# A long convolution by FFT beside a state-space scan on one core: the inner FFT stages in smaller array pieces, with real and imaginary parts on the same partition

## The chip, the cores and the metric

One core of one Trainium2 chip. The time is device microseconds of one launch. The profile that is quoted is one execution of its own: its span is the time from its first to its last instruction, and its device time stands beside it in the table.

## What is computed

Two independent layers on sequences of S = 2048 rows and D = 1024 channels; their outputs stand side by side in the last dimension.

```python
# layer A (H3): shift convolution, gate, long convolution through an FFT, gate
k_shift = sum(k_pad[:, t:t + S, :] * shift_k[:, 3 - t] for t in range(4))
kv = k_shift * v
y  = irfft(rfft(kv, 2 * S) * rfft(ssm_k, 2 * S))[:S] + kv * ssm_D
a  = q * y
# layer B (S5): a diagonal complex state-space model, P = 1024 states
Bu = x @ B_bar.T;   h[t] = Lam_bar * h[t - 1] + Bu[t]
b  = 2 * real(h @ C.T) + x * Dskip
out = concatenate([a, b], -1)
```

## The kernel before

All of the kernel's work is cut into small tasks with short names (`U`, `am`, `sh`, ...), functions in the table `E`. One long string, `ORDER`, lists about 1240 calls of them (`am.4.1` is `am(4, 1)`). The program is issued in just that order: it is the order on each engine's queue. After a colon the string names the buffers that a task takes: `p0`, `p1` (one PSUM bank each), `d0` to `d2` (PSUM tiles of two banks), `b`, `a` (SBUF ring buffers of 2 and 4 KB a partition), `m` (a product buffer), `e` (`hab`, in three copies), `w` (weights `wts`, in two copies). `@G` puts a transfer on GpSimd's queue in place of SyncE's, `@S` the other way, `@D` a copy on VectorE in place of ScalarE.

Layer B. `bl` loads blocks of B, `bT` transposes them on TensorE (L458), `bc` copies them to SBUF. `x` and `cx` load `x` and C through transposing transfers on SyncE (L483, L480). For each of 16 chunks of 128 rows, `U` multiplies with B (L492, 2048 matmuls of 128 columns), `ue` evicts, and VectorE runs a chain that cannot be split between chunks: `r1` (rotate), `r2` (add), `sc` (scan, L523), `cm` (carry), `r3`, `r4`. Then `y` multiplies with C (L546, 512 columns), with the skip term at L551, `ye` evicts and `yst` stores. Before all that the small tasks `p32` to `par_rest`, `z1`, `stt`, `rt` make tables from Lambda and dt.

Layer A. The FFT has length 4096 = 128 x 32, half of the input being zero padding.
- `kp`, `vp` load k and v; `kvm`, `kva`, `kvb`, `kvc` form kv on VectorE (L583 to L604). `wb`, `wbe` make the shift weights.
- First stage: `am` (L610) multiplies kv with the DFT matrix `F1t`, two matmuls of 128x128 by 512 columns, `ae` evicts, `ast` stores to the DRAM buffer `Ys_kv`. For the filter: `hl` loads, `hT` transposes, `hm` (L643) multiplies, `he`, `hst` store to `Ys_h`.
- Second stage, for 16 groups `gq` of two frequencies: `lh`, `lk` load from the DRAM buffers, `lw` the weights. `sh`, `sk` (`s2`, L676) multiply, `she`, `ske` evict into `hab` and `x16`. The real part of a frequency then lies on 32 partitions, the imaginary part on the next 32. `sw` makes a copy of `hab` with the two exchanged: four SBUF-to-SBUF transfers of 32 partitions. `pr` (L704) multiplies both copies with `x16` on VectorE. `sa` (L717) combines the products and does the inverse second stage in the same matmuls, `sae` evicts, `vst` stores to `Vs`.
- Last stage: `vl` loads from `Vs`, `a3` (L744) multiplies with `Gt`, `a3e` evicts, `qm` multiplies with q (loaded by `qp`), `ost` stores.

`s2` and `sa` work on pieces of 64 rows by 64 columns of the array: `tile_position` gives the piece, and four pieces with different weights can be at work together. All other matmuls use the whole array. A partition holds a block of 16 rows of the sequence, in order. Half of the entries of `F1t` and `Gt` are zero, since even and odd blocks are transformed apart from each other.

Of the kernel before, what the change touches and what calls it, by code (L numbers as in the profile page):

```python
# [18 lines left out]
MAGIC = 12582912.0  # L19
# [8 lines left out]
def a_constants():  # L28
# [13 lines left out]
    WF = np.zeros((2, N2, 2, 32, 3, N2))  # L42
# [3 lines left out]
    WF[:, :, :, :, 2, :] = WF[:, :, :, :, 0, :]  # L46
    WI = np.zeros((2, 2, N2, 16, 2, 2, N2, 2))
    for gi in range(2):
        for ui in range(2):
            for gq in range(16):  # L50
                cc = np.transpose(c_[ui, 2 * gq + gi], (1, 0)); ss = np.transpose(s_[ui, 2 * gq + gi], (1, 0))
                o = WI[gi, :, :, gq, ui]
                o[0, :, 0, :, 0] = cc; o[0, :, 0, :, 1] = ss
                o[1, :, 0, :, 0] = -cc; o[1, :, 0, :, 1] = -ss
                for cp in range(2):
                    o[cp, :, 1, :, 0] = -ss; o[cp, :, 1, :, 1] = cc
    W = np.concatenate([WF.reshape(128, NWP, 4 * 96), WI.reshape(128, NWP, 2 * 256)], axis=2)
    f = lambda a: np.ascontiguousarray(a.reshape(128, -1), dtype=np.float32).astype(ml_dtypes.bfloat16)
    return f(F1), f(G1), f(W)
# [3 lines left out]
NA = 11  # L63
# [3 lines left out]
ld_par bl.4.0@G:b0 bl.5.0@G:b1 bl.5.1@G:b2 bl.4.1:b3 bl.6.0:b4 bl.2.1@G:b5 ld_sd@S bl.1.1@G:b6 ld_w@S:a0a1 kp.0@G kp.-2 ld_F par_T:p0 hl.2@G:a2  # L67
bl.7.0:b7 bT.4.0:p1 p32 exp1 bl.6.1:b8 hl.3@G:a3 bc.4.0 dve2 x.0:b9 kp.-1@G bT.5.0:p0 dve3 sm_pre bT.4.1:p1 bc.5.0 hl.1@G:a4 bl.0.1:b10 bc.4.1
bl.7.1@G:b11 x.4:b12 bT.6.0:p0 tabA1:a5a6a7a8 bc.6.0 bl.2.0:b13 hl.0:a9 exp2 bl.0.0:b0 sin0 rt@G kp.1 bT.1.1:p1 x.2:b1 bT.5.1:p0 tabA2 bc.1.1 cx.4.1
wb.7:p1 bc.5.1 par_rest vp.0@G:a10 ld_G@S sin2 wb.4:p0 cx.5.1 wbe.4 sin1 wb.6:p0 cx.0.0 wbe.6@D eo.0 bl.3.1:b3 wb.1:p0 wbe.7@D bl.1.0:b4 wbe.1@D  # L70
wb.2:p1 cx.0.1 eo.1 stt.0 wb.0:p0 cx.7.0 wbe.2 stt.1 eo.3 wb.5:p1 bl.3.0:b6 x.1:b2 wbe.5@D wbe.0 stt.3 wb.3:p1 wbe.3 bT.6.1:p0 cx.1.0 dd bT.2.0:p1
kvm.0:m0 vp.1:a1 vp.2:a0 cx.6.0 bc.6.1 cx.6.1 bT.0.1:p0 bc.2.0 bc.0.1@D kp.2@G eo.2 bT.2.1:p1 kva.0 hT.0.0:p0 hc.0.0:b8 stt.2 bc.2.1 hT.0.1:p0
bT.7.1:p1 hc.0.1:b13 kvb.0:a7 bc.7.1 hT.0.6:p0 hm.0.0.1:d0 kvc.0 hc.0.6:b10 hT.0.3:p1 hm.0.0.0:d1 kvm.4:m0 he.0.0.1:b5 am.1.1:d2 hc.0.3:b11
hm.0.6.1:d0 hst.0.0.1 hT.0.2:p0 bT.0.0:p1 he.0.6.1:b8 hc.0.2:b0 hst.0.6.1@S cx.1.1 bc.0.0 bT.7.0:p0 bc.7.0@D cx.3.1 z1 U.0.3.0:p1 kva.4 hm.0.6.0:d0
U.0.3.1 cx.3.0 U.0.2.0:p0 kvb.4:a8 U.0.2.1 ue.0.3:a10 he.0.6.0:b7 kvm.2:m0 bT.1.0:p1 bc.1.0 am.0.1:d0 bT.3.0:p1 ue.0.2 bc.3.0 bT.3.1:p0 bc.3.1
U.0.0.0:p1 U.0.0.1 he.0.0.0:b5 kp.4@G kva.2 kp.3@G ae.0.1:b10 hm.0.3.1:d1 U.2.2.0:p0 ue.0.0 ast.0.1@S vp.4:a5 kvc.4 U.0.1.0:p1 ae.1.1:b4 cx.5.0
# [70 lines left out]
def full_kernel(ctx, tc, A_q, A_k, A_v, A_shift_k, A_ssm_k, A_ssm_D, B_x, B_Lre, B_Lim, B_Bre, B_Bim,  # L147
# [676 lines left out]
```

## Time and profile before

| | |
|---|---|
| Device time, median of 3 runs | 378.24 us (374.16 to 381.8) |
| Device time of the profiled execution | 380.41 us |
| Its span | 378.5 us |
| TensorE busy (matmuls) | 346.6 us (92%) |
| VectorE busy | 324.6 us (86%) |
| ScalarE busy | 264.2 us (70%) |
| GpSimd busy | 81.3 us (21%) |
| DMA | 100.06 MB in 67418 packets, 264 GB/s |

A busy share is a mean over the whole span. Busy times of matmuls are those of overlapping instructions with modelled ends: for the pace of a stream, starts are compared with starts. Where a row of the timeline ends in brackets, the first number is how long the engine sat idle before the row, and behind the arrow stands what it waited for. The granted TensorE clock was 1.00 throughout.

### The profile page before, as it was taken

The page shows a single profiled execution, that of the slowest core. Times are in us where ns is not written, and L with a number is a line of the kernel's source. Part 1 is how long each engine was busy: PE and PEld are TensorE (multiplying, and loading weights), DVE is VectorE, ACT ScalarE, POOL GpSimd, SP SyncE. Part 2 cuts the span into 40 slices and gives each one's busy share as a digit, 9 for nine tenths or more (in the row PEclk, how much of TensorE's full clock was granted, in tenths as well). Part 3 has the DMA queues.
Part 4 walks back from the last instruction along what each step waited for, and adds up shares of the span by engine and source line. Part 5 has one row for each costly group of instructions (what it writes and reads, how often), then busy time and mean ns, then how long its engine had stood idle before and what let it go on. Part 6 is the DMA issues. An engine that isn't in the chain of part 4 may idle for free.

```text
span 378.5 us, 8748 instructions
## 1 busy us (share of the span) xinstructions
PE 346.6 (92%) x3661; PEld 225.6 (60%) x3661; DVE 324.6 (86%) x229; ACT 264.2 (70%) x341; POOL 81.3 (21%) x150
## 2 busy tenths in 40 slices
PE   4548889899899999999999999989999999999995
PEld 3226678785455578855444757367867664467442
DVE  6989599999999997999997797576899999993972
ACT  4978798877778886952785879778869771346433
POOL 7300023022112521214200325330210202211021
PEclk9999999999999999999999999999999999999999
DMA  6999999997578999999999897999989539877995
GB/s 231 317 338 216 265 272 286 296 314 235 200 243 270 247 313 287 281 272 268 190 275 312 258 324 234 220 267 221 284 236 312 175 125 325 306 229 255 350 319 206
DMA packets 67418, 100.06 MB, mean 264 GB/s; under 512 B 38435, under 2 KB 42147, under 8 KB 67380
## 3 DMA queue, kind: packets, MB, share of 16 engines
q1 hardware_dynamic: 54660, 56.32, 54.8%
q0 software_dynamic: 12720, 43.19, 36.8%
q8 instruction: 28, 0.46, 0.5%
q14 instruction: 10, 0.08, 0.1%
HBM read 49.16 MB, written 33.55 MB: 219 GB/s over the span
## 4 chain that ended last, share of the span: by engine, by line
PE 56%; DMA 15%; issue 13%; ACT 7%; SPq 4%; POOL 2%; DVE 1%; POOLq 0%; ACTq 0%; DVEq 0%
PE ps_u L492 22%; PE ps_y L546 16%; PE ps_a L744 4%; DMA wts<-a_c_W 4%; SPq L483 4%; DMA Ys_kv<-ysb 3%; PE ps_a L643 3%; DMA l2k<-Ys_kv 3%; DMA ld<-in_B_B_re_dram 3%; PE ps_a L717 3%; PE ps_a L610 3%; DMA hab<-hab 2%; PE ps_a L676 2%; PE ps_t L630 2%; ACT ysb L615 2%
## 5 line engine op out<-in xcount | busy, mean ns | idle before, releaser
L492 PEld LDWEIGHTS <-BT 128*128 128x128 bf16 x2048 | 119.3, 98 | 22.6 <-issue 11.7
L492 PE MATMUL ps_u<-xT,BT 128*128 128x128 bf16 x2048 | 127.7, 219 | 2.4 <-ACT u L497 1.2
L546 PE MATMUL ps_y<-CT,h 128*128 128x512 bf16 x512 | 127.7, 379 | 0.0
L546 PEld LDWEIGHTS <-h 128*128 128x128 bf16 x512 | 44.6, 98 | 48.0 <-issue 6.1
L523 DVE TENSOR_TENSOR_SCAN h<-rtab,h 128x2080 bf16<-128x2080 f32 x16 | 71.8, 4488 | 0.2
L497 ACT CAST u<-ps_u 128x512 bf16<-128x512 f32 x64 | 38.2, 603 | 27.0 <-PE ps_u L492 19.1
L506 DVE TENSOR_TENSOR mt<-u,Z 128x4096 bf16<-128x4096 bf16 x16 | 36.7, 2291 | 15.8 <-ACT u L497 15.4
L704 DVE TENSOR_TENSOR hab<-x,hab 128x4096 bf16<-128x4096 bf16 x16 | 36.5, 2286 | 15.2 <-DMA hab<-hab 10.5
L556 ACT CAST yo<-ps_y 128x512 bf16<-128x512 f32 x32 | 19.1, 596 | 28.0 <-PE ps_y L546 24.4
L650 ACT CAST ysbh<-ps_a 128x1024 bf16<-128x1024 f32 x32 | 32.3, 1033 | 8.8 <-PE ps_a L643 7.5
L691 ACT CAST x<-ps_a 128x1024 bf16<-128x1024 f32 x32 | 31.9, 1026 | 8.8 <-PE ps_a L676 5.9
L506 DVE TENSOR_TENSOR mt<-h,Z 128x4096 bf16<-128x4096 bf16 x16 | 36.7, 2292 | 0.5
L724 ACT CAST vsb<-ps_a 128x1024 bf16<-128x1024 f32 x32 | 31.7, 1027 | 6.5 <-PE ps_a L717 6.0
L583 DVE TENSOR_TENSOR mt<-kring,wbc 128x2048 bf16<-128x2048 bf16 (+3 forms) x14 | 35.8, 2592 | 0.4 <-ACT wbc L473 0.2
L615 ACT CAST ysb<-ps_a 128x1024 bf16<-128x1024 f32 x32 | 32.3, 1043 | 2.7 <-issue 1.6
L685 ACT CAST hab<-ps_a 128x1024 bf16<-128x1024 f32 x32 | 32.2, 1030 | 2.1 <-PE ps_a L676 1.9
L551 PE MATMUL ps_y<-Dd,xT 128*128 128x128 bf16 x128 | 28.0, 219 | 0.0
L749 ACT CAST ot<-ps_a 128x1024 bf16<-128x1024 f32 x16 | 15.7, 1018 | 14.1 <-PE ps_a L744 14.1
L169 POOL DMA_DIRECT2D Ys_h<-ysbh x20 | 14.3, 716 | 43.3 <-ACT ysbh L650 43.3
L168 POOL DMA_DIRECT2D hab<-hab x32 | 15.6, 494 | 32.1 <-ACT hab L685 18.3
L458 PE MATMUL ps_t<-ident,ld 128*128 128x128 bf16 x128 | 13.9, 285 | 9.1 <-DMA ld<-in_B_B_re_dram 4.4
L643 PE MATMUL ps_a<-hT,F1t 128*128 128x512 bf16 x64 | 20.6, 402 | 0.8 <-ACT ysbh L650 0.6
(116 smaller groups left out, 381.8 us busy)
## 6 DMA issues: line engine op xcount, KB each, us to landing
Ys_h<-ysbh POOLq DMA_DIRECT2D x20, 256.0 KB, 5.5
l2h<-Ys_h SPq DMA_DIRECT2D x9, 512.0 KB, 9.7
Vs<-vsb SPq DMA_DIRECT2D x9, 512.0 KB, 4.3
vv<-Vs SPq DMA_DIRECT2D x9, 512.0 KB, 5.2
Ys_kv<-ysb POOLq DMA_DIRECT2D x17, 256.0 KB, 6.2
l2k<-Ys_kv SPq DMA_DIRECT2D x8, 512.0 KB, 3.9
hab<-hab SPq DMA_DIRECT2D x32, 128.0 KB, 5.4
l2k<-Ys_kv POOLq DMA_DIRECT2D x8, 512.0 KB, 7.8
```

The costliest lines, as they stand in the source:

```text
L492: nc.tensor.matmul(pu[:, w, jl, :], BT[:, 2 * jp + jl, w, d, :], xT[:, d, :], start=(d == 0), stop=(d == ND - 1))
L497: nc.scalar.copy(u[:, :, 2 * jp:2 * jp + 2, :], st["pu", i, jp][:])
L506: nc.vector.tensor_mul(m, s_, w_)
L523: nc.vector.tensor_tensor_scan(gf, rtab[:].rearrange("p a j t -> p (a j t)"), gf, 0.0, ALU.mult, ALU.add)
L546: nc.tensor.matmul(py[:], h[:, 1 - w, j, 2:TP], CT[:, j, w, dh * 512:(dh + 1) * 512], start=(j == 0 and w == 0), stop=(j == NJ - 1 and w = ...
L583: nc.vector.tensor_mul(m[:, :, j0:j0 + n, :], a_, wbc[:, j0:j0 + n, :].unsqueeze(1).to_broadcast([P, 2, n, DV]))
L615: nc.scalar.copy(st["ysb", r, u][:], st["pa", r, u][:].rearrange("p e d -> p (e d)"))
L643: nc.tensor.matmul(pd[:, e, :], F1t[:, u, :], st["hT", f, rp][:, e, :], start=True, stop=not sk)
L650: nc.scalar.copy(st["yh", f, rp, u][:], st["pa", f, rp, u][:])
L685: nc.scalar.copy(hab[:, a, :, e * 512:(e + 1) * 512], st["ps", key, gq, e][:])
L691: nc.scalar.copy(x16[:, :, e * 512:(e + 1) * 512], st["ps", "k", gq, e][:])
L704: nc.vector.tensor_mul(hab, x16.unsqueeze(1).to_broadcast([P, 2, 2 * D]), hab)
```

## The change

The blocks of 16 rows are now put on partitions by parity: even blocks on partitions 0 to 63, odd blocks on 64 to 127. `am` so needs only the nonzero halves of its matrix, in pieces of 64x64; `a3` uses pieces of 128 rows by 64 columns. In the second stage a matmul of `s2` gives the real or the imaginary part alone, in pieces of 64 rows by 32 columns, so that both parts of a frequency lie on the same partition (in different places of it). `pr` forms the four products from that, `sw` is gone, and `sa` combines four products in place of two, in pieces of 32 rows by 64 columns, both halves of the channels in one task with two PSUM tiles. Transfers whose rows are split by parity become two of 64 partitions (`kp`, `vp`, `qp`, `ost`), and `vl` is two tasks. The weight tile `wts` grows from 896 to 1024 columns. The small parameter tasks work on real and imaginary parts together, in fewer operations. There is one more ring buffer `a` (`NA` 12 for 11; the row `sd` moves into a `b` buffer), and `ORDER` is a new string throughout.

```diff
-NA = 11
+NA = 12
 ...
-    F1t = const.tile([P, 2, P], BF16, name="F1t")
-    Gt = const.tile([P, 2, P], BF16, name="Gt")
+    F1t = const.tile([P, 384], BF16, name="F1t")
+    Gt = const.tile([P, 2, 64], BF16, name="Gt")
-    kr = k.rearrange("(n s) d -> n s d", s=NR)
+    kr = k.rearrange("(n h s) d -> h n s d", h=2, s=NR)      # vr, qr, oar in the same way
 ...
     def vp(r):
         st["v", r] = k4("v", [P, 2, D])
-        spd(st["v", r][:], vr[:, 2 * r:2 * r + 2, :])
+        for h in range(2):
+            spd(st["v", r][64 * h:64 * h + 64, :, :], vr[h, :, 2 * r:2 * r + 2, :])   # kp, qp, ost in the same way
 ...
-    def am(r, u):
-        for e in range(2):
-            nc.tensor.matmul(pd[:, e, :], F1t[:, u, :], kvt(r)[:, r % 2, e * 512:(e + 1) * 512], start=True, stop=True)
+    def am(r, e):
+        for h in range(2):
+            hp = slice(64 * h, 64 * h + 64)
+            for u in range(2):
+                nc.tensor.matmul(pd[64 * u:64 * u + 64, h, :], F1t[hp, 256 + 64 * u:320 + 64 * u],
+                                 kvt(r)[hp, r % 2, e * 512:(e + 1) * 512], start=True, stop=True, tile_position=(64 * h, 64 * u))
 ...
-    def s2(key, nm, gq, e, o):
+    def s2(key, nm, gq, ri):
         for gi in range(2):
-            for u in range(2):
-                up = slice(64 * u, 64 * u + 64)
-                b0 = ((2 * gq + gi) % 4) * 96 + 32 * o
-                nc.tensor.matmul(pd[64 * gi:64 * gi + 64, u, :], wt[up, b0:b0 + 64],
-                                 st[nm, gq][up, gi, e * 512:(e + 1) * 512], start=True, stop=True,
-                                 tile_position=(64 * u, 64 * gi))
+            b0 = ((2 * gq + gi) % 4) * 64 + 32 * ri
+            for e in range(2):
+                c_ = 32 * (2 * gi + e)
+                for u in range(2):
+                    up = slice(64 * u, 64 * u + 64)
+                    nc.tensor.matmul(pd[c_:c_ + 32, u, :], wt[up, b0:b0 + 32], st[nm, gq][up, gi, e * 512:(e + 1) * 512],
+                                     start=True, stop=True, tile_position=(64 * u, c_))
 ...
-    def sw(gq):
-        hab = st["hab", gq]
-        for b in range(4):
-            o = b ^ 1
-            spd(hab[32 * b:32 * b + 32, 1, :, :], hab[32 * o:32 * o + 32, 0, :, :])
 ...
     def pr(gq):
-        nc.vector.tensor_mul(hab, x16.unsqueeze(1).to_broadcast([P, 2, 2 * D]), hab)
+        nc.vector.tensor_mul(hab, hab[:, :, 1:2, :].to_broadcast([P, 2, 2, D]), x16.unsqueeze(1).to_broadcast([P, 2, 2, D]))
 ...
-    def sa(gq, e):
-        for a in range(2):
-            for u in range(2):
-                for gi in range(2):
-                    gp = slice(64 * gi, 64 * gi + 64)
-                    b0 = 4 * 96 + (gq % 2) * 256 + u * 128 + a * 64
-                    nc.tensor.matmul(pd[64 * u:64 * u + 64, gi, :], wt[gp, b0:b0 + 64],
-                                     hab[gp, a, u, e * 512:(e + 1) * 512], start=(a == 0), stop=(a == 1),
-                                     tile_position=(64 * gi, 64 * u))
+    def sa(gq):
+        pds = [dtile("ps_a") for _ in range(2)]
+        for a, b, n in ((0, 0, 0), (0, 1, 2), (1, 0, 2), (1, 1, 1)):
+            for gi in range(2):
+                for e in range(2):
+                    cp = slice(32 * (2 * gi + e), 32 * (2 * gi + e) + 32)
+                    for u in range(2):
+                        b0 = 4 * 64 + (gq % 2) * 384 + u * 192 + n * 64
+                        nc.tensor.matmul(pds[e][64 * u:64 * u + 64, gi, :], wt[cp, b0:b0 + 64], hab[cp, a, b, u, :],
+                                         start=(a + b == 0), stop=(a + b == 2), tile_position=(32 * (2 * gi + e), 64 * u))
 ...
     def a3_(r):
         for e in range(2):
-            for u in range(2):
-                nc.tensor.matmul(pd[:, e, :], Gt[:, u, :], st["vv", r][:, u, e * 512:(e + 1) * 512], start=(u == 0), stop=(u == 1))
+            for h in range(2):
+                nc.tensor.matmul(pd[64 * h:64 * h + 64, e, :], Gt[:, h, :], st["vv", r][:, h, e * 512:(e + 1) * 512],
+                                 start=True, stop=True, tile_position=(0, 64 * h))
```

The first words of the order strings, as far as the prediction speaks of them:

```diff
-ld_par bl.4.0@G bl.5.0@G bl.5.1@G bl.4.1 bl.6.0 bl.2.1@G ld_sd@S bl.1.1@G ld_w@S kp.0@G kp.-2 ld_F par_T hl.2@G bl.7.0 bT.4.0 p32 exp1 bl.6.1
-hl.3@G bc.4.0 dve2 x.0 kp.-1@G bT.5.0 dve3 sm_pre bT.4.1 bc.5.0 hl.1@G bl.0.1 bc.4.1 bl.7.1@G x.4 bT.6.0 tabA1 bc.6.0 bl.2.0 hl.0 exp2 bl.0.0 sin0 rt@G kp.1 ...
+ld_par bl.4.0@G bl.4.1@G ld_sd kp.-1 bl.2.0@G bl.6.1 bl.7.0@G bl.2.1 bl.6.0@G bl.7.1 bl.5.0 ld_F kp.0 par_T ld_w bT.4.0 p32 hl.2 exp1 hl.0 dd dve2
+bl.1.1@G kp.1 dve3 bl.5.1@G sm_pre vp.0 hl.1@G kp.-2@G bl.0.0 bT.2.0 bc.4.0@D bl.1.0 tabA1 bT.4.1 bc.2.0 bl.0.1 exp2 bT.7.0 sin0 rt@G ... hl.3@G ... x.0 ...
```

More of the change, by code (lines that the diff above doesn't have):

```diff
@@ L69 @@
[L69 to L76, printed above, removed]
@@ L754, in full_kernel, with ost @@
     E["qm"] = qm
-    E["ost"] = lambda r: gpd(oar[:, r, :], st["ot", r][:])
+    def ost(r):
+        for h in range(2):
+            gpd(oar[h, :, r, :], st["ot", r][64 * h:64 * h + 64, :])
+    E["ost"] = ost
     with tc.manual_schedule():
```

328 lines of the change are left out of this document (162 added, 166 removed).

## The prediction

> **What bounds the kernel now.** I read the page first (busy shares), then the windows (how the shares move over the span), the groups of lines, the TensorE timeline, and the chain.
>
> ```profile
> span 378.5 us, 8748 instructions
> PE 346.6 (92%) x3661; PEld 225.6 (60%) x3661; DVE 324.6 (86%) x229; ACT 264.2 (70%) x341; POOL 81.3 (21%) x150
> ...
> PE   4548889899899999999999999989999999999995
> ...
> PE 56%; DMA 15%; issue 13%; ACT 7%; SPq 4%; POOL 2%; DVE 1%; POOLq 0%; ACTq 0%; DVEq 0%
> ```
> ```profile
> 0.00:20.00 20.00, 9.48 (x55) 5.66 (x56) 16.40 (x50) 14.26 (x23) 10.56 (x25) 1.00 0.87 273
> 20.00:40.00 20.00, 13.77 (x84) 8.73 (x84) 17.79 (x21) 14.57 (x28) 1.27 (x2) 1.00 1.12 279
> ...
> 100.00:150.00 50.00, 48.94 (x471) 32.22 (x470) 46.58 (x28) 40.36 (x49) 13.41 (x22) 1.00 0.86 255
> ...
> 200.00:250.00 50.00, 48.87 (x592) 29.67 (x591) 37.64 (x20) 39.40 (x49) 15.80 (x31) 1.00 0.94 276
> ...
> 360.00:378.50 18.50, 14.65 (x76) 6.73 (x73) 8.80 (x12) 6.20 (x8) 3.25 (x6) 1.00 0.76 265
> ```
> In a window row the figures after the length are PE, PEld, DVE, ACT and POOL busy, then granted clock, DMA share and GB/s. TensorE is busy 48.9 of 50 us in the middle and idles for 10.52 + 6.23 = 16.7 us only in the first 40. VectorE is close behind it up to 150 us (46.58 of 50), but has 12.4 us of room between 200 and 250. The chain is 56% PE and 1% DVE. So from about 44 us to the end the order of TensorE's work is the time: what leaves its stream leaves the span, and what only shortens a wait of VectorE does not.
>
> **The change part by part: what TensorE streams.** Busy times of matmuls overlap, so I take start to start.
>
> ```profile
> 142.52 0.86 PE ps_a L610 x4
> ...
> 317.76 2.16 PE ps_y L546 x10
> ...
> 323.38 0.86 PE ps_a L744 x4
> ```
> ```profile
> 301.81 1.96 PE L492 MATMUL ps_u<-xT,BT 128*128 128x128 bf16 x32
> 303.61 0.38 PE L546 MATMUL ps_y<-CT,h 128*128 128x512 bf16 x1
> ...
> 304.58 1.06 PE L492 MATMUL ps_u<-xT,BT 128*128 128x128 bf16 x16
> 305.57 1.06 PE L717 MATMUL ps_a<-hab,wts 64*64 64x512 bf16 x16
> 306.56 0.39 PE L546 MATMUL ps_y<-CT,h 128*128 128x512 bf16 x1
> ```
> A 512-column stream takes 2.16/10 = 0.216 us, and four of L610 or L744 take 0.86. The 16 tiled matmuls of L717 (two `sa` words, each 8 matmuls on four 64x64 array pieces) take 306.56 − 305.57 = 0.99 us: one after the other they would take 16 x 0.216 = 3.5, as packs of four 4 x 0.216 = 0.864. So four pieces run as one stream, and 0.99 − 0.86 = 0.12 is left over. Ahead of them 32 plain `U` matmuls take 303.61 − 301.81 = 1.80, 56 ns each; the 16 before `sa` take 0.99 in place of 0.90. So going from the full array to pieces costs about 0.09 us and coming back 0.12, about 0.105 a transition.
>
> ```profile
> L610 PE MATMUL ps_a<-acc,F1t 128*128 128x512 bf16 x64 | 19.0, 387 | 0.4 <-ACT ysb L615 0.2 <-ACT ysbh L650 0.2
> L717 PE MATMUL ps_a<-hab,wts 64*64 64x512 bf16 x256 | 18.2, 383 | 0.8 <-DVE hab L704 0.7
> L744 PE MATMUL ps_a<-vv,Gt 128*128 128x512 bf16 x64 | 16.1, 379 | 0.0
> ...
> L676 PE MATMUL ps_a<-l2h,wts 64*64 64x512 bf16 x128 | 11.3, 387 | 3.0 <-DMA wts<-a_c_W 2.3 <-DMA l2h<-Ys_h 0.7
> L676 PE MATMUL ps_a<-l2k,wts 64*64 64x512 bf16 x128 | 10.8, 385 | 0.0
> ```
> - `am` (L610): 64 full streams become 128 pieces of 64x64, that is 32 packs of four: 32 x 0.216 less, **−6.9 us**. The shape is the one that L717 runs now.
> - `a3` (L744): 64 full streams become 64 of 128 rows by 64 columns, two side by side. Bounds: 0 if the two halves take turns, −6.9 if they run together. Nearest is the pack of four, which contains two column pieces: I take **−6.9**.
> - `sh`/`sk` (L676): 256 pieces of 64x64 become 512 of 64 rows by 32 columns; `sa` (L717): 256 become 512 of 32 rows by 64 columns. In packs of eight that is 64 packs each, as many as the packs of four now. Bounds: 0 if eight run as one stream, 2 x 64 x 0.216 = +27.6 if they need two passes; below nothing is excluded, since the number of streams is the same. I take **0**, by the pack of four, in which a second, third and fourth piece add nothing that can be seen.
> - Transitions. Counting the PE words of the two order strings, the array changes its division 78 times before (39 visits) and 144 times after: `am`, `sh`/`sk`, `sa` and `a3` each have a division of their own, and one is entered straight from another only 6 times. 66 x 0.105 = **+6.9 us**. Bounds for the divisions not seen here: 0 (then −6.9 + 0) to twice the price, 144 x 0.21 − 78 x 0.105 = +22.0. I take the measured one.
>
> TensorE's stream so changes by −13.8 + 6.9 = −6.9 us, all in stages where it is the bound.
>
> **The start.** The first `U` comes at 44.11 us.
>
> ```profile
> 11.70 1.89 PE L458 MATMUL ps_t<-ident,ld 128*128 128x128 bf16 x16 [2.48 <-DMA ld<-in_B_B_im_dram]
> ...
> 26.83 1.89 PE L458 MATMUL ps_t<-ident,ld 128*128 128x128 bf16 x16 [3.68 <-DMA ld<-in_B_B_re_dram]
> ...
> 44.11 1.05 PE L492 MATMUL ps_u<-xT,BT 128*128 128x128 bf16 x16 [0.31 <-ACT BT L473]
> ```
> ```profile
> 6.99 4.90 SPq L483 DMA_TRANSPOSE xT<-in_B_x_dram  x1
> ...
> 12.71 8.41 SPq L483 DMA_TRANSPOSE xT<-in_B_x_dram  x1
> ```
> ```profile
> 43.84 0.69 DVE L469 COPY BT<-ps_t 128x1024 bf16<-128x1024 bf16 x1 [4.28 <-PE ps_t L458]
> ```
> SyncE is held by the transposing loads `x.0` and `x.4` for 4.90 and 8.41 us; the loads `bl` queued behind them come late, and TensorE waits 2.48 + 3.68 = 6.2 us for them. In the new order thirteen words of plain loads on SyncE (`bl`, `hl`, `kp`, `vp`) stand ahead of `x.0`, and no second transpose stands among them. VectorE loses 4.28 us because `bc.0.1@D` is queued ahead of `kva.0`; after, no such copy stands between `kvm.0` and `kva.0`. Eleven `bT` rather than 13 stand ahead of the first `U`, but these are only moved. Against it: `hl.3@G` now stands behind `rt@G` on GpSimd, and the first `hT` needs all four `hl`.
>
> ```profile
> 12.57 2.02 POOL L471 COPY rtab<-r 128x1024 f32<-128x1024 f32 x2
> ```
> ```profile
> hk<-in_A_ssm_k_dram POOLq DMA_DIRECT2D x4, 512.0 KB, 11.4
> ```
> With `rt` ending near 14.6 us and 11.4 to land, `hl.3` is there at about 26 us (an estimate); the first `hT` was at 29.8 before, so this needn't cost. DMA was at a share of 1.12 there, so not all 6.2 us can come back. Bounds: −8 (both waits and part of VectorE's) to +4 (the reordered loads collide); I take two thirds of 6.2, **−4**. The parameter arithmetic has 21 small VectorE operations for 31, 10 x 0.17 = 1.7 us, and three more `bc` but two fewer `wbe` on VectorE (+2.1 − 1.4); they lie in this start, and I book no more for them.
>
> ```profile
> L330 DVE TENSOR_TENSOR br<-lbr,p 128x8 f32<-128x8 f32 x1 | 0.2, 168 | 0.0
> ```
>
> **The exchange and the transfers.**
>
> ```profile
> hab<-hab SPq DMA_DIRECT2D x32, 128.0 KB, 5.4
> ...
> hab<-hab POOLq DMA_DIRECT2D x32, 128.0 KB, 7.0
> ```
> ```profile
> L704 DVE TENSOR_TENSOR hab<-x,hab 128x4096 bf16<-128x4096 bf16 x16 | 36.5, 2286 | 15.2 <-DMA hab<-hab 10.5 <-ACT x L691 4.6
> ...
> L168 POOL DMA_DIRECT2D hab<-hab x32 | 15.6, 494 | 32.1 <-ACT hab L685 18.3 <-DMA l2k<-Ys_kv 13.6 <-ACT x L691 0.2
> ```
> ```profile
> 256.34 0.84 PE L676 MATMUL ps_a<-l2h,wts 64*64 64x512 bf16 x12 [1.81 <-DMA wts<-a_c_W]
> ```
> `sw` goes: 64 transfers, 8.4 of 100 MB. `pr` keeps its 4096 elements a partition, so 2.29 us each, and loses 10.5 us of waiting; VectorE has room there, so this is not on the path except where `sa` waited for `pr` (0.7). Split in two are `kp` (r ≥ 0), `vp`, `qp` and `ost`, and `vl` is two words: 8 + 8 + 8 + 16 + 16 = 56 issues more. GpSimd then issues 141 for 138, SyncE 176 for 187; at 0.494 us a GpSimd issue three more cost 1.5 us, covered by an engine 21% busy. If a queue were full in the last stage, 18 `vl` and 18 `ost` issues there would cost it 18 us of a stage of 60: still cover. The weight tile grows from 224 to 256 KB: its reload already stalls TensorE by 1.81 once, and one reload (`lw.2`, five PE words ahead of `sh.4.0`) stays short. For waits in the middle I take **−1** (bounds −3 to +5).
>
> **Sum.** The profiled execution took 380.41 us, 1.9 of it around the span. 380.41 − 6.9 − 4 − 1 = 368.5. It was 2.2 above the median of the runs (378.24), so on that scale: **366.3**, 3.2% faster.
>
> **Rivals.**
> (1) *A pack of eight costs more than one stream.* In two passes: +27.6, 366.3 + 27.6 = **393.9**, slower. It decides from the point where 12/27.6 = 43% of the packs need a second pass. Loads of weights could do it as well: eight in place of four must hide behind 0.216 us.
>
> ```profile
> 305.57 0.58 PEld L717 LDWEIGHTS <-wts 64*64 64x64 bf16 x16
> ```
> Sixteen loads fit into 0.58 us here, 36 ns each: eight at that rate are 0.29, +0.07 x 64 = +4.7 for `sa`; if the loads here only waited for room behind the packs (0.58 us is most of three packs), nothing. For it: no row shows eight. Against it: four cost no more than one. Chance 0.13. [...]
> (2) *Transitions into the new divisions cost double.* +22.0 for +6.9: **381.4**, no change. For it: 144 of them, three divisions unseen. Against it: in and out cost nearly the same now. Chance 0.10.
> (3) *VectorE sets the pace up to 200 us.* Then `am`'s part (−6.9 + 46 x 0.105 = −2.1) and half of the start's are void: 366.3 + 2.1 + 2 = **370.4**. For it: 46.58 of 50 us. Against it: the chain is 1% DVE, and its own stall of 4.28 goes. Chance 0.15.
> (4) The forecast, 366.3, its own range 359 to 373: 0.62.
>
> **How the numbers follow.** About 2% (370.7 to 385.8) is what a measurement of this kernel tells from no change. Faster: 0.56 of the forecast and 0.07 of (3) = 0.63. Same: 0.06 of the forecast, 0.08 of (3), 0.08 of (2) = 0.22. Slower: (1) and 0.02 of (2) = 0.15. The range takes in the start at −8 and the waits at −3 (360), a little of free transitions below that, and above it (3) and (2): 358 to 383.
>
> **What would show it.** Right: no `hab` transfer; four `am` matmuls in 0.22 us start to start, `a3` four in 0.43; 32 matmuls of `sa` in 0.86 + 0.2; the first `U` at about 40 us; PE busy about 10 us lower. Wrong: an `sa` word of 1.7 us or more (1); U words after a pack late by 0.2 or more (2); waits of TensorE for `u` or `hab` products of VectorE, with VectorE idle nowhere before 200 us (3); TensorE idle in the first 40 us as before.

## The result: slower by 4%, and the profile after

The changed kernel took 391.57 us (median of 4 runs, 390.84 to 393.88), beside 376.20 for the kernel before on the same chip (median of two; all its four runs lie from 374.16 to 386.24). The ratio is 1.042, 95% interval 1.030 to 1.054. Executions of one and the same kernel fall into a fast and a slow group some per cent apart, and the medians, ranges and ratios given here are those of the fast ones. The kernel before scatters most, from 371.7 to 388.4 us over all its executions, so a ratio to it is known to a per cent or two only. The forecast was 366.3, in a range of 358 to 383. The profiled execution took 390.84 us.

The page of the changed kernel (busy shares, the strips of 40 slices, the packets, the chain):

```profile
span 389.1 us, 9800 instructions
PE 342.4 (88%) x4196; PEld 223.6 (57%) x4237; DVE 324.3 (83%) x220; ACT 263.5 (68%) x340; POOL 84.3 (22%) x153
...
PE   1668467599998999999999999999999999969996
...
PEclk9999699589999999999999999999999999998999
...
DMA packets 65555, 92.01 MB, mean 236 GB/s; under 512 B 38394, under 2 KB 41994, under 8 KB 65512
...
PE 62%; DMA 22%; ACT 7%; issue 7%; SPq 1%; POOL 1%; POOLq 0%; ACTq 0%
```

TensorE is busy 4.2 us less than before, in a span 10.6 us longer. The digits of its strip say where the rest went: 4, 6, 7 and 5 in the slices from 39 to 78 us, where before there were 8s and 9s, and a 6 near 345 us. DMA's part of the chain rose from 15 to 22%. The same in windows of 100 us, first the kernel before, then the changed one (columns as in the prediction's windows):

```profile
0.00:100.00 100.00, 77.98 (x829) 57.90 (x830) 89.09 (x98) 76.73 (x109) 23.44 (x46) 1.00 1.03 278
```
```profile
0.00:100.00 100.00, 66.37 (x702) 51.41 (x710) 73.68 (x83) 62.47 (x92) 26.98 (x53) 0.91 1.07 223
...
20.00:40.00 20.00, 15.10 (x83) 8.01 (x82) 17.49 (x25) 15.25 (x28) 3.66 (x7) 1.00 1.16 206
40.00:60.00 20.00, 11.40 (x151) 10.62 (x153) 12.60 (x6) 11.68 (x15) 3.58 (x6) 0.83 1.07 202
60.00:80.00 20.00, 13.00 (x137) 10.35 (x135) 14.34 (x8) 9.51 (x12) 2.92 (x5) 0.74 1.14 205
```

In the first 100 us TensorE does 11.6 us less work, and VectorE and ScalarE lose even more (15.4, 14.3): nothing replaced TensorE as the bound, everything waited. The last two columns name the place. DMA's engines are busy a little more than before (1.07 for 1.03) and move a fifth less (223 for 278 GB/s): the transfers became slower, not fewer. The DMA issues of these 100 us (KB each, median us from issue to landing), first of the kernel before:

```profile
kring<-in_A_k_dram POOLq DMA_DIRECT2D x4, 512.0 KB, 6.9
hk<-in_A_ssm_k_dram SPq DMA_DIRECT2D x4, 512.0 KB, 7.6
ld<-in_B_B_re_dram SPq DMA_DIRECT2D x6, 256.0 KB, 4.3
CT<-in_B_C_im_dram SPq DMA_TRANSPOSE x8, 7.5
```
```profile
hk<-in_A_ssm_k_dram SPq DMA_DIRECT2D x3, 512.0 KB, 18.0
kring<-in_A_k_dram SPq DMA_DIRECT2D x5, 256.0 KB, 20.5
ld<-in_B_B_re_dram SPq DMA_DIRECT2D x4, 256.0 KB, 17.8
CT<-in_B_C_im_dram SPq DMA_TRANSPOSE x8, 17.2
```

Of what stands on SyncE's queue, these groups land some 10 us and more later, also those that the change left whole (`hk` 18.0 for 7.6, `ld` 17.8 for 4.3, `CT` 17.2 for 7.5); not all do: the loads `ld` of the imaginary part take 8.0 for 6.9, `CT` of the real part 5.6 for 6.9. (How much of this is the new order and how much the halves, the runs with whole transfers tell.) Who waited for it, in the view of waits (us in total, times, longest), and what that did to TensorE, in its timeline:

```profile
DVE mt L575 <- DMA kring<-in_A_k_dram: 7.4, 1, 7.4
...
PE ps_t L447 <- DMA ld<-in_B_B_re_dram: 5.6, 2, 4.5
...
PE ps_a L732 <- DMA vv<-Vs: 3.0, 2, 2.3
```
```profile
45.18 1.89 PE L481 MATMUL ps_u<-xT,BT 128*128 128x128 bf16 x16 [5.76 <-DMA xT<-in_B_x_dram]
...
62.44 0.41 PE L604 MATMUL ps_a<-acc,F1t 64*64 64x512 bf16 x4
62.78 0.90 PE L481 MATMUL ps_u<-xT,BT 128*128 128x128 bf16 x13
...
286.70 1.07 PE L705 MATMUL ps_a<-hab,wts 32*64 32x512 bf16 x32
287.70 0.41 PE L673 MATMUL ps_a<-l2k,wts 64*32 64x512 bf16 x8
...
356.06 1.49 PE L732 MATMUL ps_a<-vv,Gt 128*64 128x512 bf16 x12
357.48 3.75 PE L481 MATMUL ps_u<-xT,BT 128*128 128x128 bf16 x64
```

How a late load of v stops TensorE, three rows of the timeline show. VectorE's last step of kv (`kvc.4`, L596) waits for `v`. ScalarE's `ae.1.1` (L610) waits for VectorE, since it writes into the ring buffer in which that `v` lies (`vp.2:a6` and `ae.1.1:a6` in the order string). TensorE's next `hm` (L638) waits for `ae`, which empties the PSUM tile that `hm` needs.

```profile
65.49 1.22 DVE L596 TENSOR_TENSOR acc<-acc,v 128x2048 bf16<-128x2048 bf16 x1 [5.98 <-DMA v<-in_A_v_dram]
...
66.87 1.93 ACT L610 CAST ysb<-ps_a 128x1024 bf16<-128x1024 f32 x2 [3.31 <-DVE acc L596]
...
67.93 0.59 PE L638 MATMUL ps_a<-hT,F1t 128*128 128x512 bf16 x2 [2.71 <-ACT ysb L610]
```

The first `U` came at 45.18 in this profile, not at 40. After 5.76 us of idling its 16 matmuls took 1.89 us, where they took 1.05 in the kernel before:

```profile
44.11 1.05 PE L492 MATMUL ps_u<-xT,BT 128*128 128x128 bf16 x16 [0.31 <-ACT BT L473]
```

The granted clock had dropped: in windows of 2 us it stands at 0.50 from 44 to 48 us and from 70 to 78, and at 1.00 from 50 to 68; over the windows of 40 to 80 us that is 0.83 and 0.74, where it was 1.00 before. By these shares, a loss of about 11.4 x 0.17 + 13.0 x 0.26 = 5 us on top of the waiting (an estimate). Both drops begin in a wait of TensorE or just after one; but waits of 2.48 and 3.68 us in the kernel before left its clock at 1.00, so that the waits bring the drops about is not shown.

The other rows of the timeline show the part that went as forecast. An `am` word of four pieces takes 62.78 − 62.44 = 0.34 us start to start, one stream of 0.216 and 0.12 for the change of division. The 32 matmuls of `sa` take 1.00, four streams and 0.14 for the change to the division of `sk`. Twelve `a3` matmuls take 1.42: six pairs of 0.216 and 0.12. The groups agree (us busy): `am` 11.6 for 19.0, `a3` 9.5 for 16.1, `sa` 18.1 for 18.2 with twice the matmuls.

```profile
L705 PE MATMUL ps_a<-hab,wts 32*64 32x512 bf16 x512 | 18.1, 380 | 0.4 <-ACT vsb L711 0.4
...
L604 PE MATMUL ps_a<-acc,F1t 64*64 64x512 bf16 x128 | 11.6, 397 | 0.1
...
L732 PE MATMUL ps_a<-vv,Gt 128*64 128x512 bf16 x64 | 9.5, 416 | 3.0 <-DMA vv<-Vs 3.0
```

### The profile page after: what moved, and what is told of

It reads as the page before. It is cut to its first block, busy times and chain, and to the rows that moved or that the text cites. A ratio compares the mean times of both kernels' runs of the same rounds, so it can differ in the third digit from the quotient of the medians.

```text
span 389.1 us, 9800 instructions
## 1 busy us (share of the span) xinstructions
PE 342.4 (88%) x4196; PEld 223.6 (57%) x4237; DVE 324.3 (83%) x220; ACT 263.5 (68%) x340; POOL 84.3 (22%) x153
## 4 chain that ended last, share of the span: by engine, by line
PE 62%; DMA 22%; ACT 7%; issue 7%; SPq 1%; POOL 1%; POOLq 0%; ACTq 0%
PE ps_u L481 26%; PE ps_y L535 20%; DMA hk<-in_A_ssm_k_dram 5%; DMA xT<-in_B_x_dram 4%; PE ps_a L705 4%; DMA Ys_h<-ysbh 3%; PE ps_a L673 3%; DMA vv<-Vs 3%; PE ps_a L638 2%; DMA l2k<-Ys_kv 2%; PE ps_a L604 2%; PE ps_a L732 2%; DMA Vs<-vsb 2%; ACT ysb L610 2%; DMA kring<-in_A_k_dram 2%
## 5 line engine op out<-in xcount | busy, mean ns | idle before, releaser
L481 PE MATMUL ps_u<-xT,BT 128*128 128x128 bf16 x2048 | 130.2, 223 | 11.8 <-DMA xT<-in_B_x_dram 5.8
L481 PEld LDWEIGHTS <-BT 128*128 128x128 bf16 x2048 | 121.5, 100 | 29.1 <-issue 17.7
L535 PE MATMUL ps_y<-CT,h 128*128 128x512 bf16 x481 | 123.0, 379 | 2.4 <-issue 1.1
L486 ACT CAST u<-ps_u 128x512 bf16<-128x512 f32 x64 | 37.7, 597 | 19.9 <-PE ps_u L481 16.1
L691 DVE TENSOR_TENSOR hab<-hab,x 128x4096 bf16<-128x4096 bf16 x16 | 36.6, 2286 | 14.8 <-ACT x L685 12.7
L495 DVE TENSOR_TENSOR mt<-u,Z 128x4096 bf16<-128x4096 bf16 x16 | 36.6, 2290 | 11.8 <-ACT u L486 11.3
L610 ACT CAST ysb<-ps_a 128x1024 bf16<-128x1024 f32 x32 | 31.9, 1029 | 10.2 <-PE ps_a L604 6.9
L645 ACT CAST ysbh<-ps_a 128x1024 bf16<-128x1024 f32 x32 | 31.9, 1024 | 10.0 <-PE ps_a L638 3.1
L685 ACT CAST x<-ps_a 128x1024 bf16<-128x1024 f32 x32 | 31.9, 1024 | 7.7 <-PE ps_a L673 6.5
L738 ACT CAST ot<-ps_a 128x1024 bf16<-128x1024 f32 x16 | 15.8, 1016 | 18.3 <-PE ps_a L732 14.2
L447 PE MATMUL ps_t<-ident,ld 128*128 128x128 bf16 x128 | 14.1, 281 | 10.6 <-DMA ld<-in_B_B_re_dram 5.6
L638 PE MATMUL ps_a<-hT,F1t 128*128 128x512 bf16 x54 | 18.0, 402 | 5.4 <-ACT ysb L610 4.4
L168 POOL DMA_DIRECT2D Ys_h<-ysbh x18 | 13.0, 725 | 41.6 <-ACT ysbh L645 39.6
L447 PEld LDWEIGHTS <-ld 128*128 128x128 bf16 x128 | 11.8, 129 | 15.2 <-issue 9.0
```

The lines of the kernel that those rows point to most:

```text
L481: nc.tensor.matmul(pu[:, w, jl, :], BT[:, 2 * jp + jl, w, d, :], xT[:, d, :], start=(d == 0), stop=(d == ND - 1))
L486: nc.scalar.copy(u[:, :, 2 * jp:2 * jp + 2, :], st["pu", i, jp][:])
L495: nc.vector.tensor_mul(m, s_, w_)
L535: nc.tensor.matmul(py[:], h[:, 1 - w, j, 2:TP], CT[:, j, w, dh * 512:(dh + 1) * 512], start=(j == 0 and w == 0), stop=(j == NJ - 1 and w = ...
L610: nc.scalar.copy(ysb[:, :, e * 512:(e + 1) * 512], st["pa", r, e][:])
L645: nc.scalar.copy(st["yh", f, rp, u][:], st["pa", f, rp, u][:])
```

## The experiments

Theory H1: a transfer that touches only partitions 0 to 63, or only 64 to 127, moves at a much lower rate, and `kp`, `vp`, `qp`, `ost`, `vl` and `ast` (which stores two times 64 partitions as well) became such halves; `kp` for r < 0 did too, whose two transfers covered 112 and 15 partitions before and cover 64 and 63 now. Rivals: H2, the number of issues; H3, the new order at the start. The kernel before ran beside each of them, with medians of 374.2 to 379.1 us. The runs stand on several chips.

**b_halves and b_evenodd: only the splitting, put into the kernel before.**

```diff
 # in kp (r >= 0), vp, qp, vl and ost of the kernel before; vp stands for all
-        spd(st["v", r][:], vr[:, 2 * r:2 * r + 2, :])
+        for z in (slice(0, 64), slice(64, 128)):            # b_evenodd: slice(0, 128, 2), slice(1, 128, 2)
+            spd(st["v", r][z, :, :], vr[z, 2 * r:2 * r + 2, :])
```

> The kernel before with one thing changed: each k, v, q load, each load of Vs and each store of the long convolution's output is issued as two transfers, partitions 0 to 63 and 64 to 127, with the same data in the same places (56 more issues, same packets and bytes). Theory H1, a transfer that touches only one half of the partitions moves at a much lower rate: 388 to 395 us, 3% or so over before, with the k and Vs loads landing late and GB/s lower in the first 100 us. Rival H2, the extra issues and their place in the queues: the same slowing here as in the run with even and odd partitions. Rival H3, the new order at the start: no change here, 377 to 382 us.

> The control to the run with halves: the same loads and stores are issued as two transfers each, one of the even partitions and one of the odd ones, so issues, packets, bytes and order are the same, but each transfer spreads over the whole height of the partitions. H1 (halves are slow because they touch one half): within 1% of before, 376 to 384 us. H2 (more issues): as slow as the run with halves. H3 (the new order at the start): no change, as in the run with halves.

Measured: halves 391.06 us (389.68 and 392.43, ratio to before 1.023, interval 1.012 to 1.034); even and odd partitions 376.46 (375.94 to 379.46, ratio 0.987, 0.978 to 0.996). Same issues, packets and bytes, 15 us apart. Their first 100 us, halves and then even and odd:

```profile
0.00:100.00 100.00, 67.75 (x775) 52.10 (x776) 79.79 (x93) 70.11 (x101) 23.40 (x46) 0.85 1.05 251
```
```profile
0.00:100.00 100.00, 76.70 (x828) 57.25 (x829) 91.09 (x99) 76.52 (x109) 26.08 (x51) 0.97 1.04 278
```

The halves alone slow the kernel before by 2 to 4% (4% beside the even and odd ones), with the marks of the changed one: fewer GB/s (251 for 278) at the same share of DMA (1.05 for 1.03), TensorE 10 us short (67.8 for 78.0), the clock down (0.85 for 1.00). 56 more issues cost nothing that can be seen (b_evenodd, ratio 0.987). H2 falls; H3 is not needed for the loss.

**m_halves: the transfers alone.** 4 MiB a phase.

> Transfers alone, nothing of the reference computed: 4 MiB of k into a tile in seven phases, each after the one before is complete: (1) 8 transfers of 128 partitions by 4 KB on SP's queue, (2) 16 of 64 partitions on SP, lower and upper half in turn, (3) 16 of even and odd partitions on SP, (4) lower halves on SP and upper on POOL, (5) whole ones on SP and POOL in turn, (6) all lower halves, then all upper ones, (7) as phase 1; then 4 MiB stored whole and 4 MiB stored in halves. H1: phases 2 and 6 take 1.5 to 2 times phase 7, phase 3 as long as phase 7, phase 4 in between or as phase 7. H2: phases 2 and 3 are alike and longer than phase 7 by the 8 more issues, some 0.1 us each. H3: all phases alike.

The nine phases as windows (length, VectorE and GpSimd busy, clock, DMA share, GB/s):

```profile
0.70:13.40 12.70, 0.00 (x0) 0.00 (x0) 1.00 0.85 330
13.40:33.80 20.40, 0.21 (x2) 0.00 (x0) 1.00 0.87 206
33.80:48.90 15.10, 0.14 (x1) 0.00 (x0) 1.00 0.80 278
48.90:67.20 18.30, 0.18 (x2) 4.19 (x8) 1.00 0.84 229
67.20:80.30 13.10, 0.18 (x2) 2.15 (x4) 1.00 0.83 320
80.30:103.10 22.80, 0.17 (x2) 0.00 (x0) 1.00 0.89 184
103.10:116.70 13.60, 0.21 (x2) 0.00 (x0) 1.00 0.92 336
116.70:127.00 10.30, 0.13 (x1) 0.00 (x0) 1.00 0.96 371
127.00:146.00 19.00, 0.19 (x1) 0.00 (x0) 1.00 0.72 221
```

Halves take 20.4 us where whole transfers take 12.7 (phase 1) and 13.6 (phase 7): 1.5 to 1.6 times. Phase 7 isn't the clean one, since the first stores go out within it: 336 GB/s in 13.6 us are more than its own 4.19 MB. So the rate of whole loads is the 330 GB/s of phase 1. Even and odd partitions take 15.1, 11 to 19% over whole ones where H1 had expected nothing. Halves in one go, all lower and then all upper, are slower still (22.8). Little is gained when the other half is under way as well: with one half on each of two queues it is still 18.3 against 13.1. Stores lose as much, 221 GB/s for 371. In phase 2 the DMA engines are as busy as in phase 1 (0.87, 0.85): the same 4 MiB keep them busy for 0.87 x 20.4 = 17.7 us in place of 0.85 x 12.7 = 10.8. Why halves take longer, the runs do not show.

**a_whole: the changed kernel with its halves made whole.**

```diff
+    krn = k.rearrange("(n s) d -> n s d", s=NR)              # vrn, qrn, oarn in the same way
-        for h in range(2):
-            spd(st["v", r][64 * h:64 * h + 64, :, :], vr[h, :, 2 * r:2 * r + 2, :])
+        spd(st["v", r][:], vrn[:, 2 * r:2 * r + 2, :])      # kp, qp, ost in the same way
-        spd(vv[64 * u:64 * u + 64, :, :], Vs[u, r, :, :].rearrange("(h m) d -> m h d", h=2))
+        if ("vl", r) not in st:
+            st["vl", r] = 1
+            spd(vv[:], Vs[:, r, :, :].rearrange("u k d -> k u d"))
-gpd(Ys_kv[u, r, :, :].rearrange("(h m) d -> m h d", h=2), st["ysb", r][64 * u:64 * u + 64, :, :])
+gpd(Ys_kv[u, r, :, :], st["ysb", r][:, u, :])
```

> The changed kernel with its half transfers made whole: k, v, q, the outputs of the long convolution, Vs and its first exchange move as single transfers of 128 partitions, in the same order of issue and the same bytes (the rows of k, v and q are then in their natural order and the second of the two loads of Vs moves nothing, so the values are permuted). H1: the time falls to 366 to 375 us, most of the way to what was forecast, with TensorE's busy time in the first 100 us back at 75 or more. H2: about the same, since it has fewer issues as well; it's told from H1 by the pair of runs on the kernel before. H3 (the new order at the start): the time stays at 385 to 392 us.

Measured: 369.77 us (369.01 to 370.87), ratio to before 0.968 (0.960 to 0.975). Its first 100 us, and its first `U`:

```profile
0.00:100.00 100.00, 78.05 (x866) 57.77 (x867) 89.40 (x91) 76.41 (x109) 27.21 (x52) 0.98 1.00 263
```
```profile
36.99 1.05 PE L485 MATMUL ps_u<-xT,BT 128*128 128x128 bf16 x16 [0.31 <-ACT hT L631]
```

Its landing times in these 100 us:

```profile
hk<-in_A_ssm_k_dram SPq DMA_DIRECT2D x3, 512.0 KB, 9.9
...
CT<-in_B_C_im_dram SPq DMA_TRANSPOSE x8, 5.1
```

The halves cost 391.6 − 369.8 = 21.8 us (by the ratios, 1.042 and 0.968, some 28). With them whole, `hk` and `CT` land early again; `ld` and `kring` still take 14.9 and 16.4 us on SyncE's queue, which is the new order. `U` starts at 36.99, 7.1 us earlier than in the kernel before. H3 falls. That start isn't the main thing the halves spoil, though: with k and v whole it comes at 36.6 to 37.0 in all four runs; with k and v as halves in the new order it varies from 36.90 (a_whole_late) to 45.18, and a_whole_late is slow with the early one. Most of what the halves cost lies behind the first `U`.

**a_fix, a_fix_early, a_fix_late, a_fix_ast: a repair that failed.** The same rows on the same partitions, but one transfer of 128 partitions, whose rows are two runs of 64 in DRAM.

```diff
-        for h in range(2):
-            spd(st["v", r][64 * h:64 * h + 64, :, :], vr[h, :, 2 * r:2 * r + 2, :])
+        spd(st["v", r][:], vr[:, :, 2 * r:2 * r + 2, :])                        # kp, qp, ost in the same way
-        spd(vv[64 * u:64 * u + 64, :, :], Vs[u, r, :, :].rearrange("(h m) d -> m h d", h=2))
+        spd(vv[:, u, :], Vs[:, r, 64 * u:64 * u + 64, :])                       # ast likewise
```

> The changed kernel with the same rows on the same partitions, but its half transfers written as whole-height ones: a load of k, v or q and a store of the long convolution's output is one transfer whose 128 partitions are read or written in DRAM as two runs of 64 rows; the two transfers of Vs and of the first exchange each take one half of the columns' sub-sequences on all 128 partitions, where they took one half of the partitions. Nothing is left out and nothing is permuted. Theory H1 (a transfer that touches one half of the partitions is slow): 368 to 372 us, as the run with permuted whole transfers (369.8). Rival H1b, the permutation or the one missing load of Vs in that run made the gain: over 376 us.

> The changed kernel with only its k and v loads at whole height (as in the full repair; the stores and loads of the rest stay halves). H1 with the loss at the start, through loads that land late in the first 100 us: 375 to 381 us, some two thirds of the 22 us between the changed kernel and the whole transfers, and TensorE's busy time in the first 100 us at 75 or more. Rival, the loss lies with the exchange and the end (Vs, q, outputs): 386 to 392 us.

> The changed kernel with only the loads of Vs and q and the stores of the long convolution's output at whole height (k, v and the first exchange's stores stay halves). H1 with the loss at the start: 384 to 389 us, the waits for Vs at 340 to 360 us gone (2 to 4 us) and the first 100 us as they were. Rival, the loss lies late: under 380 us.

> The changed kernel with only the stores of the first exchange (32 of 256 KB) at whole height. H1: these go out from 47 us on, through the queues in which the loads of the first 100 us stand, so 385 to 391 us, with less waiting for the buffers of the ysb tiles; if the stores were what delays the loads, under 380 us.

Measured: 642.97, 466.63, 487.46 and 493.74 us. All four expectations were wrong, and the runs say nothing on where the halves cost; the new form was far worse than the halves.

**m_forms: why.**

> Transfers alone, nothing of the reference computed: 4 MiB of k into a tile in eight phases, each after the one before is complete: (1, 2) 8 whole transfers on SP, (3) 16 halves on SP, (4) 16 transfers of 128 partitions by 2 KB on SP, one per row, (5) 8 whole ones on SP whose 128 partitions are two runs of 64 rows in DRAM (the form of the repair that failed), (6) whole on POOL, (7) halves on POOL, (8) the two-run form on POOL; then 4 MiB stored in the two-run form on SP. If the two-run form is what made the repair slow: phases 5 and 8 take over 2 times phases 2 and 6, POOL's the most; if it is the queues' order in the kernel, phases 5 and 8 are as long as 2 and 6. H1: phase 3 is 1.5 times phase 2, phase 7 likewise against phase 6, and phase 4 (as many issues, whole height) within 15% of phase 2.

Phases 4 to 8 and the stores:

```profile
46.80:60.70 13.90, 0.20 (x2) 0.00 (x0) 1.00 0.87 302
60.70:143.90 83.20, 0.14 (x2) 0.00 (x0) 1.00 0.12 50
143.90:157.40 13.50, 0.14 (x2) 4.38 (x8) 1.00 0.80 311
157.40:177.30 19.90, 0.20 (x2) 8.14 (x16) 1.00 0.88 211
177.30:202.60 25.30, 0.14 (x2) 6.32 (x8) 1.00 0.86 173
202.60:282.80 80.20, 0.17 (x1) 0.00 (x0) 1.00 0.13 50
```

The form it is, not the queues' order. On SyncE the two runs take 83.2 us, six times the 13.9 of 16 whole-height transfers of the same bytes, at a DMA share of 0.12: by that share, 0.12 x 16 = 1.9 of the profile's 16 engines at work in the mean (an estimate). On GpSimd they take 25.3 for 13.5, with the engines as busy as ever (0.86 for 0.80), less than the factor of 2 that was expected, and not the worse of the two. Halves on GpSimd take 19.9 for 13.5, the 1.5 of SyncE. And 16 transfers of whole height take 13.9 us for the 12.8 of 8 (phase 2, 328 GB/s; 16 halves in phase 3 take 20.6): it is the height that counts, hardly the number (1.1 us for 8 issues more, 0.14 each). Why the two runs are slow, and why so differently on the two queues, was not shown.

**a_whole_in, a_whole_late, a_whole_ast: which halves cost.** The edits of a_whole for `kp` and `vp` only, for `qp`, `ost` and `vl` only, and for `ast` only.

> The changed kernel with only its k and v loads as plain whole transfers (rows in their natural order, so the values are permuted; all else as in the changed kernel). H1 with most of the loss at the start: 374 to 380 us, that is 11 to 17 of the 21.8 us between the changed kernel and the run with all transfers whole, first U at 40 us or earlier. Rival, the loss lies with Vs, q, the outputs or the first exchange: 386 to 391 us.

> The changed kernel with only q, the outputs of the long convolution and Vs as plain whole transfers (the second load of Vs moves nothing and q's and the outputs' rows are permuted; k, v and the first exchange stay halves). H1 with most of the loss at the start: 384 to 388 us, with TensorE's 340 to 360 us full again and the first 100 us as slow as in the changed kernel. Rival, the late halves carry the loss: under 380 us.

> The changed kernel with only the 32 stores of the first exchange as whole transfers (rows of the exchange permuted, all else as in the changed kernel). H1, with the halves of k and v as the main loss: 385 to 391 us; if the half stores delay the loads of the first 100 us: under 383.

Measured: 374.67 (373.22 to 376.12), 388.97 (387.41 to 392.53) and 387.24 us (386.14 to 390.91), with ratios to before of 1.002, 1.031 and 1.022. From 391.57 that is 16.9, 2.6 and 4.3 us; by the ratios, from 1.042, about 15, 4 and 7. Either way the k and v loads are by far the largest part, and they are only 9 of 92 MB (36 transfers of 256 KB or little less): 22 of them go out in the first 100 us, in which DMA is full (a share of 1.07). The first two runs stood on one chip. Their windows from 40 to 80 us, a_whole_in and then a_whole_late:

```profile
40.00:80.00 40.00, 33.65 (x471) 28.46 (x476) 37.96 (x20) 29.58 (x37) 10.02 (x16) 0.96 1.03 233
```
```profile
40.00:80.00 40.00, 23.80 (x252) 19.15 (x254) 24.11 (x13) 17.94 (x23) 6.50 (x11) 0.74 1.14 196
```

Here is the loss: with k and v as halves TensorE works 23.8 us of these 40 (24.4 in the changed kernel), with k and v whole 33.7. With halves VectorE waits 9.8 us for `kring`, ScalarE's `ae` 7.4 for the step of VectorE that takes `v`, and TensorE 5.3 in one go for `ae` (in the changed kernel that step waits 5.98 for `v`, `ae` 3.31 and TensorE 2.71). With k and v whole, VectorE idles 1.1 us before its reads of `kring` and ScalarE 6.9 before `ae`, 0.9 and 6.7 of it for other things (`wbc`, TensorE), and TensorE waits for `ae` 1.1 in one go. The late halves, 16 MB, show in a wait (`a3` for `vv`, 3.0 us in the changed kernel, none in a_whole_late), but cost little by themselves: a_whole_late lies a little above its range of 384 to 388.

**a_whole_full: the price of the array pieces.**

```diff
 # a_whole, and am and a3 on the full array
-        for h in range(2):
-            hp = slice(64 * h, 64 * h + 64)
-            for u in range(2):
-                nc.tensor.matmul(pd[64 * u:64 * u + 64, h, :], F1t[hp, 256 + 64 * u:320 + 64 * u], ...)
+        for u in range(2):
+            nc.tensor.matmul(pd[:, u, :], F1t[:, u * P:(u + 1) * P], kvt(r)[:, r % 2, e * 512:(e + 1) * 512], start=True, stop=True)
...
-                nc.tensor.matmul(pd[64 * h:64 * h + 64, e, :], Gt[:, h, :], st["vv", r][:, h, e * 512:(e + 1) * 512], ...)
+                nc.tensor.matmul(pd[:, e, :], Gt[:].rearrange("p h m -> p (h m)"), st["vv", r][:, h, e * 512:(e + 1) * 512],
+                                 start=(h == 0), stop=(h == 1))
```

> The run with all transfers whole, and besides with the two steps am and a3 on the full array again (two and four matmuls of 512 columns of 128 by 128 each, as in the kernel before, for four pieces; the values are not the reference's). It prices the array pieces on their own: streams of 13.8 us more and the transitions of 96 packs fewer. If the prediction's term holds (6.9 us net of transitions for the whole change, all on the path): 376 to 382 us against 369.8. If TensorE is not what sets the time there: under 373 us. If pieces cost nothing extra at their edges: 383 us.

Measured: 375.98 us (375.17 to 379.79), at the lower edge of the expected, 6.2 more than a_whole. By the prediction's prices, 13.8 of streams minus the transitions saved (144 before the edit, 84 after it, 60 x 0.105 = 6.3; the packs saved are 64, not 96) is 7.5. So TensorE sets the time, and the term has the right size. It isn't known closer than to a few us: the two runs stood on different chips, and by their ratios (0.968, 0.997) the difference is some 11 us.

**a_mix: a version that computes the reference, with k and v whole.** k and v are loaded whole, in natural order, so `am` is on the full array, and `ast` is whole; `a3` and `sa` keep their pieces, `vl`, `qp` and `ost` their halves (the edits of `kp`, `vp` and `ast` from a_whole, that of `am` from a_whole_full).

> The changed kernel with the k and v loads and the stores of the first exchange whole, rows in natural order, and therefore the step am on the full array (two matmuls of 512 columns, for four pieces), as in the kernel before; everything is computed, and sa and a3 keep their array pieces and the halves of Vs, q and the outputs. From the runs: 375.0 (k and v whole) plus about half of the 6.2 us that am and a3 on the full array cost, minus what the first exchange's whole stores give (0 to 5): 373 to 378 us, against some 379 before and 391 for the changed kernel. If the gain of the whole loads needed the array pieces of am beside it: over 382.

Measured: 374.61 us (371.25 to 376.04, 12 runs) beside 378.28 for the kernel before; ratio 0.990, interval 0.986 to 0.994. That is 1% faster than the kernel before, clear of its interval, but less than the 2% that the prediction took as what a measurement of this kernel tells. Since nothing is permuted here, the permutation in the runs with whole transfers isn't what made their gain. It keeps the new order, `pr` without the exchange and the pieces of `a3`, and gives up the saving of `am` for whole loads. Its first 100 us:

```profile
0.00:100.00 100.00, 78.34 (x845) 58.57 (x846) 90.52 (x92) 77.35 (x111) 27.73 (x52) 0.90 0.97 267
```

## Why the prediction was wrong, by its steps

- *What bounds the kernel:* right from 100 us on (TensorE busy 96.0, 98.4 of 100 us after the change). But the first 44 us were read as a place with slack to win, not as the place where the kernel is bound by transfers (DMA's share was 0.99 in the first 40 us before, 0.88 and 1.16 in the two halves of them after). And "what only shortens a wait of VectorE does not" count, from about 44 us on, fails where such a wait is long: VectorE's wait for v until 65 us (5.98) stopped TensorE (2.71) through a ring buffer.
- *TensorE's stream, −6.9:* right. `am` and `a3` lost 7.4 and 6.6 us of busy time, packs of eight run as one stream (the four packs of an `sa` word in 1.00 us with the change of division), leaving a pack costs 0.12 to 0.14 where 0.12 was read, and the pieces of `am` and `a3` bring 6.2 us (by the ratios 11) where the same prices give 7.5.
- *The start, −4 (bounds −8 to +4):* wrong as measured, first `U` at 45.18 in place of 40. Its own mechanism was right and too small: with k and v whole, `U` starts at 36.6 to 37.0 in the new order, against 40.9 to 44.4 in the three runs of the old one.
- *The exchange and the transfers:* **the step that failed.** It counted the split of `kp` (r ≥ 0), `vp`, `qp`, `ost` and `vl` as 56 issues more, and booked nothing for them, since GpSimd's 0.494 us each are covered. That issues cost nothing is right: b_evenodd has the same 56 and is no slower (ratio 0.987). But the term was the wrong one. What the halves changed is the rate of their bytes, 330 to 206 GB/s by themselves, and the step had no term for it; `ast` and `kp` for r < 0, which became halves too, weren't named as such. The −1 for waits, bounds −3 to +5, came out as about +20: 391.6 − 369.8 = 21.8 for all halves, most of it for k and v.
- *Rivals.* (1) packs in two passes: false, `sa` takes 1.00 a word of 32. (2) transitions double: false. (3) VectorE sets the pace: false; in the first 100 us it waits for `kring` and `v` itself and is 15.4 us less busy than before, and from 100 to 200, where it is busy 96.2, TensorE is never seen to wait for it. The rival of two passes named nearly the right time (393.9) for a reason that is not there; a rival of slower transfers was missing.
- *What would show it:* "TensorE idle in the first 40 us as before" came true (23.2 us busy of 40, as before), and from 40 to 80 it was worse.

Without the halves the total comes out: 368.5 was forecast for the profiled execution, and that of a_whole took 369.65. That it does so this closely is in part luck: its start gave 7.1 us for the 4 booked, so the rest gave about 4 less than its sum, and the kernel before scatters by more than that. So the failed step, with the drop of the clock that came along with its waits (0.83 and 0.74 from 40 to 80 us), accounts for the miss. Not settled is how much of the 21.8 us is the clock alone; no run kept the waits and the clock apart.

## What to carry to other kernels

Price a transfer by the rows of partitions that it reaches, not by its issue: one over 64 adjacent partitions ran here at 0.6 to 0.7 of the rate, on either queue (206 GB/s for 330 on SyncE's, 211 for 311 on GpSimd's) and with the other half under way beside it (229 for 320), and in the changed kernel whole transfers on the same queue landed later (`hk` 18.0 us for the 9.9 of a_whole, `CT` 17.2 for 5.1). Then look at what takes the buffers of a late load next: that is how a wait of VectorE reached TensorE here. Look first at the stage where DMA is full (a share of 1.07 here): k and v, 9 MB of halves that go out mostly there, cost 15 to 17 us, 16 MB later on cost 3 to 4. When an edit splits a tensor by partition halves, test the splitting alone in the old kernel, with an even and odd split beside it as a control.

## What the runs showed of the hardware

- Halves (m_halves): 206 GB/s for 330 in loads, 221 for 371 in stores, 229 for 320 with two queues at work, one half on each; every other partition, 278.
- A transfer of 128 partitions whose DRAM side is two runs (m_forms): 50 GB/s on SyncE's queue, 173 on GpSimd's.
- Eight array pieces, of 64 by 32 or 32 by 64, take one stream's time like four (32 matmuls of `sa` in 1.00 us, the 8 of an `sk` 0.23 start to start with the next word, the 16 of two old `sa` 0.99), and 32-row pieces cost hardly more at their edges than 64-row ones (0.14 and 0.12 us).
